# The seven-product second layer for two more token blocks of an attention and mixture-of-experts kernel

## The chip, the core and the metric

The kernel runs on one core of one Trainium2 chip. The metric is device time in microseconds for one execution, the median of several runs. Three runs of the kernel before took 1181.03, 1179.86 and 1181.36 us.

## What is computed

Linear attention (4 batches, 8 heads, 576 tokens, head size 64) gives 2304 tokens of width 512; a mixture of four experts and then an ELU network follow. Cut to what matters:

```python
kv = einsum("bhsd,bhse->bhde", softmax_k, v); x = einsum("bhsd,bhde->bhse", softmax_q, kv)   # -> (2304, 512)
for e in range(4):
    out += p[:, e:e+1] * (np.maximum(x @ w1[e], 0) @ w2[e])          # 512 -> 1024 -> 512
h = out @ w_in                                                        # float64 weights, 512 -> 2048
g = np.where(h > 0, h, np.exp(np.minimum(h, 0)) - 1.0)
return (g @ w_out).astype(np.float32)                                 # 2048 -> 512
```

## The kernel before, in words

**Number format.** Every matrix operand is split into a high part, rounded to the matmul format, and the rest (hi by a ScalarE Copy, lo by a subtraction on VectorE or GpSimd). One product of two split operands is three matmuls.

**Units, blocks, steps.** After the attention and the first expert, the work is ten units of 512 hidden columns, s = 0 to 9: 0 to 5 are the experts 1 to 3, 6 to 9 are the ELU network (`S_MOE` = 6; "sixth" in the change's name is this s = 6). Tokens are cut into three blocks b of 768. A step is (s, b), 30 in all. In step (s, b) TensorE runs the first layer of (s, b), 14 products named idx 0 to 13 (two halves `fp` of seven, a Strassen-like scheme of 7 products in place of 8), six matmuls each, and between them, at fixed places, the second layer of the step before.

**The second layer** has two forms. Units 0 to 4 and 7 to 9 (`SEVEN`) use seven products too. For units 7 to 9 this is `turned_product`: for each of the seven products in `TURNED`, 12 matmuls of 384 columns into a pair of PSUM banks, which VectorE then adds to the result (L1321). The transposed result lies in `accs`, in quarters (th, mh). Units 5 and 6 are plain. Unit 6 does eight `group`s (L1283 to L1286): 12 matmuls of 384 columns each, and one ScalarE Copy that writes the result's first value. The seven-product form needs sums of the four weight quarters (T1 to T4) and, of the hidden layer, the seven operands A11, A22, S1 to S4, A12 in place of eight plain parts; `fast(i)` says whether step i is of that form, and `elu` makes the operands with more VectorE sums and more conversions (`parts`, L1199 to L1201).

**PSUM.** Four banks A to D take the first layer's products. ScalarE copies out of them at idx 0 and 1 of each half (L1467, L1470), VectorE adds at idx 2 and 4 (L1474, L1485), then `elu` reads them. A product waits when its bank has not been read.

**The order.** All is written out by hand. Each step has 24 hooks; `hooks` says how many have run after which product. `at2(i, k, fn)` puts work on hook k of step i; a k of 24 or more reaches into the next steps. Engines run their own instructions in the order of the program, SP (and in places ScalarE) their DMAs, so that an instruction that waits holds those behind it.

**Other work on the hooks.** (a) `convert` turns a tile of the float64 weights `w_in`, `w_out` into float32 in the DRAM buffer `scratch`: load (L467, L469), five VectorE instructions (L487 to L506), one Exp, a store (L509); `CONV` lists the places of all 32. (b) `w_load`, `w1_steps`, `w2_step`, `w2_fast` load and split the weights of the next unit; the raw tiles are two slots of the pool `stg` (tag "r"), and split second-layer weights eight slots of `wp` (tag "w2"). (c) Between units 5 and 6 the expert result is turned: `turn_steps(b, c)` transposes two rows of 128 tokens (`turn`, L970), makes the operands T1 to T4, B11 to B22 and stores them to `xs[1]` (`emit`, L988 to L999), through staging places handed out in turn by `staged`; the next step's loads (`ring_load`, L719) read them in the second half of a step. One stream per (b, c), six items, one item after each product, at most two streams at once.

**What the change touches:** `TURNED`'s constants, `w2_parts`/`w2_sum` as called by `w2_fast`, `w2_step`, `CONV`, the loop that places `w_load`, `staged`, the places of `turn_steps`, `fast`, and `turned_product`.

Of the kernel before, what the change touches and what calls it, by code (L numbers as in the profile page):

```python
# [21 lines left out]
def tile_attention_moe_moe(  # L22
# [13 lines left out]
    nc = tc.nc  # L36
# [73 lines left out]
    )  # L110
    STARTS, ENDS = (0, 1, 5), (3, 4, 5, 6)
    GROUPS = tuple((th, m) for th in (1, 0) for m in range(4))
# [705 lines left out]
    def w2_sum(s, op):  # L818
# [4 lines left out]
        nc.vector.tensor_tensor(out=o, in0=x, in1=y, op=ALU.subtract)  # L823

    def w2_fast(i, s, d):

        for k, fn, op in (
            (8, w2_parts, "B11"), (16, w2_sum, "T1"), (17, w2_parts, "T1"), (18, w2_parts, "B22"), (19, w2_sum, "T3"),
            (20, w2_parts, "B21"), (22, w2_sum, "T2"), (24, w2_parts, "T2"), (30, w2_sum, "T4"), (31, w2_parts, "T3"),
            (35, w2_parts, "T4"),  # L830
        ) if s > S_MOE else (
            (8, w2_parts, "B11"), (13, w2_sum, "T1"), (17, w2_parts, "T1"), (18, w2_parts, "B22"), (19, w2_sum, "T3"),
            (21, w2_parts, "B21"), (22, w2_parts, "T3"), (24, w2_sum, "T2"), (26, w2_parts, "T2"), (27, w2_sum, "T4"),
            (30, w2_parts, "T4"),
        ):
            put = lambda k, fn: at2(i, k, fn) if k >= 0 else at(210 + k, fn)
            put(k - d, lambda fn=fn, op=op: fn(s, op))

    def w2_step(s, p):
        r = w2r.pop((s, p))  # L840
        for j in range(2):
            t = wp.tile([P, 2, DM], F32R, tag="w2", name="w2s")
            nc.scalar.activation(out=t[:, 0], in_=r[:, j], func=AF.Copy)
            nc.gpsimd.tensor_tensor(out=t[:, 1], in0=r[:, j], in1=t[:, 0].bitcast(F32), op=ALU.subtract)
            w2s[s, 2 * p + j] = t


# [4 lines left out]
    def at2(i, k, fn):  # L852
        timed2.setdefault(i * SH + int(k), []).append(fn)
# [16 lines left out]
    for n, fn in zip((190, 191, 192, 193, 194, 195, 197, 198, 200, 201), w1_steps(0, 0).values()):  # L870
# [11 lines left out]
        (later, SPELL * n + t, d, False)  # L882
        for n in range(S_FAST) for t, d in ((10, 2), (34, 1), (48, 1), (62, 1)) if (n, t) != (0, 10)
    ]
    CONV += [(later, end1 + t, 1, True) for t in (11, 22, 33)]
    end2 = NB * S_MOE * SH
    CONV += [(later, end2 + t, 1, True) for t in (42, 56)]
    assert len(CONV) == NCONV
# [4 lines left out]
    for i, (s, b) in enumerate(STEPS):  # L893
# [7 lines left out]
        if b == 0:  # L901

            a2, b2, c2, d2, a1, b1 = (2, 13, 25, 29, 34, 38)
            if s > 0 and (s <= S_FAST or SEVEN[s]):
# [4 lines left out]
                else:  # L909
                    at2(i, 14, lambda s=s: w2_step(s, 0))  # L910
                    at2(i, 19, lambda s=s: w2_step(s, 1))
                    a2, b2, c2, d2, a1, b1 = (23, 26, 30, 34, 38, 42)
            if s == S_MOE:
                a1, b1 = (42, 42)
            elif s > S_MOE:
                a1, b1 = (35, 40)
# [12 lines left out]

    stage, more_places = ["y", "qh", "ql", "extra", "ek"], []  # L930

    def staged():
# [9 lines left out]
        if now >= -SH and not more_places:  # L942
            y = gt.rearrange("p k n -> p (k n)").bitcast(F32R)
            more_places.extend(y[:, k * DM : (k + 1) * DM].rearrange("p (l n) -> p l n", l=2) for k in range(3))
            stage[:0] = more_places
        if now >= 0 and any(isinstance(t, str) for t in stage):
            stage[:] = two(stg, "r") + [t for t in stage if not isinstance(t, str)]
        if now >= 14 and len(stage) == 7:
            stage[:0] = two(stg, "r")
        t = stage.pop(0)  # L950
# [73 lines left out]
    for b in range(NB):  # L1024
        i = NB * (S_MOE - 1) + b + 1
        for c, n in enumerate((7, SH - 1, SH + 3)):
            f = turn_steps(b, c)
# [135 lines left out]
    def fast(i):  # L1163
        return 0 <= i < len(STEPS) and SEVEN[STEPS[i][0]]

# [129 lines left out]
    def turned_product(i, k):  # L1295
# [6 lines left out]
        op, wname, (th, mh) = TURNED[k]  # L1302
        t, y = w2g[s, wname], sums["XY"[(i + k) % 2]][:, :, :TB]
        last = i + 1 == len(STEPS)
        ym = [y[:, 0], (A, C)[k % 2]] if last else [y[:, 0], y[:, 1]]
        for m in range(2):
            n = 0
            for fp in range(2):
                gh, gl = parts_of(i, op, fp)
                w = t[:, :, fp, m * P : (m + 1) * P]  # L1310
                for l, r in ((w[:, 0], gh), (w[:, 1], gh), (w[:, 0], gl)):
# [7 lines left out]
        def add(ms, x):  # L1319
            a = acc_turned(b, th, mh)[:, ms]  # L1320
            nc.vector.tensor_tensor(out=a, in0=x, in1=a, op=ALU.add)  # L1321
            if s == STEPS[-1][0] and k in ENDS:
# [284 lines left out]
```

## Time and profile before

| | |
|---|---|
| median of 3 runs | 1181.03 us (1179.86 to 1181.36) |
| the profiled execution | 1180.01 us |
| its span, first to last instruction | 1178.2 us |
| TensorE clock granted | 1.00 throughout |
| instructions | 21091 |

In the profile PE is TensorE's matmuls, PEld its weight loads (one per matmul), DVE is VectorE, ACT ScalarE, POOL GpSimd, SP the queue that issues most DMAs. L1283 is line 1283 of the kernel before. A step begins with the first weight load of its idx 0; by that, the steps begin at 635.87 us (4,1), 725.09 (5,1), 827.32 (6,1), 859.66 (6,2), 890.86 (7,0), 951.49 (7,2) and 981.25 (8,0), and each ends where the next begins. A matmul's shown time overlaps the next one's, so TensorE's pace is read from the distance of the weight loads, not from the duration of one.

### The profile page before, as it was taken

The page shows a single profiled execution, that of the slowest core. Times are in us where ns is not written, and L with a number is a line of the kernel's source. Part 1 is how long each engine was busy: PE and PEld are TensorE (multiplying, and loading weights), DVE is VectorE, ACT ScalarE, POOL GpSimd, SP SyncE. Part 2 cuts the span into 40 slices and gives each one's busy share as a digit, 9 for nine tenths or more (in the row PEclk, how much of TensorE's full clock was granted, in tenths as well). Part 3 has the DMA queues.
Part 4 walks back from the last instruction along what each step waited for, and adds up shares of the span by engine and source line. Part 5 has one row for each costly group of instructions (what it writes and reads, how often), then busy time and mean ns, then how long its engine had stood idle before and what let it go on. Part 6 is the DMA issues. An engine that isn't in the chain of part 4 may idle for free.

```text
span 1178.2 us, 21091 instructions
## 1 busy us (share of the span) xinstructions
PE 1161.9 (99%) x7551; PEld 1113.6 (95%) x7551; DVE 883.9 (75%) x1533; ACT 656.1 (56%) x1410; POOL 604.1 (51%) x582
## 2 busy tenths in 40 slices
PE   8999999999999999999999999999999999999998
PEld 6889898889999999999999999998999999999998
DVE  7878887555787787787787786576566779879876
ACT  7554544236455455455455453356767766767763
POOL 6522543027468468468468463246534645645643
PEclk9999999999999999999999999999999999999999
DMA  9446666846767767767777658798985465565462
GB/s 270 144 144 191 192 211 222 287 166 224 259 233 251 259 233 251 258 233 250 253 239 251 241 208 311 259 340 279 335 320 188 181 230 198 196 229 198 176 242 108
DMA packets 150345, 272.76 MB, mean 231 GB/s; under 512 B 12640, under 2 KB 74848, under 8 KB 150240
## 3 DMA queue, kind: packets, MB, share of 16 engines
q1 hardware_dynamic: 148512, 268.26, 66.1%
q10 hardware_dynamic: 1728, 3.15, 0.8%
q8 instruction: 60, 0.98, 0.3%
q14 instruction: 45, 0.37, 0.1%
HBM read 225.22 MB, written 46.14 MB: 230 GB/s over the span
## 4 chain that ended last, share of the span: by engine, by line
PE 80%; DVE 5%; ACT 2%; issue 1%; POOL 1%; DMA 0%; DVEq 0%; POOLq 0%; ACTq 0%
PE o L1403 19%; PE m L1177 17%; PE h L1177 17%; PE o L1312 8%; PE h L1035 4%; PE o L1035 4%; PE o L1283 1%; PE o L1284 1%; PE o L1285 1%; PE o L1264 1%; PE o L1265 1%; PE o L1263 1%; DVE accs L1321 1%; PE o L970 1%; DVE w1s L777 1%
## 5 line engine op out<-in xcount | busy, mean ns | idle before, releaser
L1177 PE MATMUL m<-xh,w1s 128*128 128x384 f32 x840 | 245.9, 337 | 1.3 <-DVE h L1474 0.8
L1177 PE MATMUL h<-xh,w1s 128*128 128x384 f32 x840 | 244.8, 337 | 1.9 <-DVE half L1233 0.9
L1177 PEld LDWEIGHTS m<-xh,w1s 128*128 128x128 f32 x840 | 154.2, 188 | 6.1 <-DVE gt L1360 2.2
L1177 PEld LDWEIGHTS h<-xh,w1s 128*128 128x128 f32 x840 | 154.8, 188 | 5.1 <-DVE half L1233 1.5
L1177 PE MATMUL h<-xl,w1s 128*128 128x384 f32 x420 | 140.7, 335 | 0.0
L1177 PE MATMUL m<-xl,w1s 128*128 128x384 f32 x420 | 140.6, 335 | 0.0
L1035 PE MATMUL o<-w2t,hpa 128*128 128x512 f32 x432 | 117.1, 399 | 1.0 <-ACT hpa L1066 0.5
L1035 PE MATMUL h<-xh,w1t 128*128 128x256 f32 (+1 forms) x512 | 110.9, 295 | 0.0
L1403 PE MATMUL o<-w2g,xh 128*128 128x256 f32 x540 | 90.4, 282 | 0.0
L1035 PEld LDWEIGHTS o<-w2t,hpa 128*128 128x128 f32 x432 | 75.7, 189 | 14.8 <-DVE hpa L1067 1.9
L1035 PEld LDWEIGHTS h<-xh,w1t 128*128 128x128 f32 x512 | 85.0, 189 | 4.8
L1403 PE MATMUL o<-w2g,hpa 128*128 128x256 f32 x540 | 89.0, 282 | 0.0
L1403 PE MATMUL o<-w2g,xl 128*128 128x256 f32 x540 | 87.3, 282 | 0.0
L815 POOL TENSOR_TENSOR w2g<-r,w2g 128x512 fp32r<-128x512 f32 x56 | 74.8, 1344 | 24.2 <-ACT w2g L814 24.2
L1425 DVE SCALAR_TENSOR_TENSOR accs<-o,pn,accs 128x256 f32<-128x256 f32 x180 | 75.7, 475 | 14.7 <-PE o L1403 14.1
L1177 PEld LDWEIGHTS h<-xl,w1s 128*128 128x128 f32 x420 | 79.2, 189 | 0.3
L1177 PEld LDWEIGHTS m<-xl,w1s 128*128 128x128 f32 x420 | 78.9, 188 | 0.5
L1403 PEld LDWEIGHTS o<-w2g,xh 128*128 128x128 f32 x540 | 78.0, 190 | 0.1
L1035 PE MATMUL h<-xl,w1t 128*128 128x256 f32 (+1 forms) x256 | 77.0, 301 | 0.5 <-DVE xl L413 0.5
L1403 PEld LDWEIGHTS o<-w2g,hpa 128*128 128x128 f32 x540 | 76.1, 190 | 0.1
L1403 PEld LDWEIGHTS o<-w2g,xl 128*128 128x128 f32 x540 | 75.7, 190 | 0.1
L1201 POOL TENSOR_TENSOR hpa<-gt,hpa 128x384 fp32r<-128x384 f32 x28 | 28.5, 1020 | 75.3 <-ACT hpa L1199 75.3
(357 smaller groups left out, 2960.3 us busy)
## 6 DMA issues: line engine op xcount, KB each, us to landing
xh<-xs SPq DMA_DIRECT2D x210, 384.0 KB, 5.5
xl<-xs SPq DMA_DIRECT2D x210, 384.0 KB, 6.1
r<-in_w_dram SPq DMA_DIRECT2D x56, 256.0 KB, 4.8
xs<-xh SPq DMA_DIRECT2D x21, 384.0 KB, 4.6
xs<-xl SPq DMA_DIRECT2D x21, 384.0 KB, 4.4
xs<-stage SPq DMA_DIRECT2D x29, 256.0 KB, 5.1
r<-scratch SPq DMA_DIRECT2D x24, 256.0 KB, 4.2
xs<-gt SPq DMA_DIRECT2D x21, 256.0 KB, 4.5
```

What stands on the lines that cost most here:

```text
L777: eng.tensor_tensor(out=dst(k, 1), in0=src(k), in1=dst(k, 0).bitcast(F32), op=ALU.subtract)
L815: nc.gpsimd.tensor_tensor(out=t[:, 1], in0=src, in1=t[:, 0].bitcast(F32), op=ALU.subtract)
L970: nc.tensor.transpose(t[:, d * P : (d + 1) * P], a[:, d * P : (d + 1) * P], ident)
L1035: nc.tensor.matmul(out, lhsT, rhs, **kw)
L1177: nc.tensor.matmul(dst, t[:, wl, c + dl, :], x[xl_][:, dl, :], start=(n == 0 and p < 2), stop=(n == 5), skip_group_check=True,)
L1201: eng.tensor_tensor(out=gl, in0=g, in1=gh.bitcast(F32), op=ALU.subtract)
L1263: nc.tensor.matmul(o, gh, w[:, 0, :], start=(f == 0), stop=False)
L1264: nc.tensor.matmul(o, gh, w[:, 1, :], start=False, stop=False)
L1265: nc.tensor.matmul(o, gl, w[:, 0, :], start=False, stop=(f == FS - 1))
L1312: nc.tensor.matmul(ym[m], l, r, start=(n == 0 and k in STARTS), stop=(n == 5), skip_group_check=True)
L1403: nc.tensor.matmul(o, l, r, start=(first_write and m == 0 and c != 1), stop=(m == 5), skip_group_check=True)
L1425: nc.vector.scalar_tensor_tensor(out=a, in0=sums[x][:, c * HALF_M : (c + 1) * HALF_M], scalar=pr, in1=a, op0=ALU.mult, op1=ALU.add)
```

## The change

Steps (6,1) and (6,2) become `fast`: their second layers, issued in steps (6,2) and (7,0), are seven products in place of eight groups. Block 0 of unit 6 stays plain, and so does all of unit 5.

- Products that are the first to write a quarter of the result (`OPENS`: the first, second, third and seventh) are written by a ScalarE Copy when s is 6; the other three are added by VectorE as in units 7 to 9.
- B11, B21, B22 are taken from the plain split tiles of unit 6 (`w2_of`). For T1 to T4, `sums_of` subtracts the raw quarters on VectorE three and four hooks after `w2_step`, in the raw tile itself, and stores it to a DRAM buffer; in step (6,1) four loads (hooks 1, 3, 5, 7) bring the sums into "w2" slots, and `sum_parts` splits them ten hooks or more later.
- Unit 7's second-layer weights are split at other hooks, so that their slots are free by then.
- Two conversions leave unit 6 (hooks 42 and 56 from its start); units 3 and 4 get five in place of four.
- The loads of unit 6's first-layer weights are issued at hooks 41 and 54 of (5,0) on, in place of 38 and 42.
- Block 2's second turn starts at hook 17 of step (6,0) in place of 23; near the end of that step `staged` gives up the three places in `gt` one by one and, from hook 4 of (6,1), all but the four places in the raw slots.

```diff
-    STARTS, ENDS = (0, 1, 5), (3, 4, 5, 6)
+    STARTS, ENDS, OPENS = (0, 1, 5), (3, 4, 5, 6), (0, 1, 2, 6)
...
+    sums_dram = nc.dram_tensor("sums", (2, P, 2, DM), F32).ap()
+    SUM_HOME = {"T1": (0, 0), "T3": (0, 1), "T2": (1, 1), "T4": (1, 0)}
+
+    def sums_of(r, j, last):
+        b11, b12, b21, b22 = (r[:, a, c * HALF_M : (c + 1) * HALF_M] for a in range(2) for c in range(2))
+        for o, x, y in ((b22, b22, b11), (b21, b21, b22)) if last else ((b11, b12, b11), (b12, b12, b22)):
+            nc.vector.tensor_tensor(out=o, in0=x, in1=y, op=ALU.subtract)
+        if last:
+            nc.sync.dma_start(out=sums_dram[j], in_=r)
+
+    def sum_load(s, op):
+        a, c = SUM_HOME[op]
+        t = wp.tile([P, 2, 2, HALF_M], F32R, tag="w2", name="w2g")
+        src = sums_dram[:, :, a, c * HALF_M : (c + 1) * HALF_M].rearrange("j p n -> p j n")
+        nc.sync.dma_start(out=t[:, 1].bitcast(F32), in_=src)
+        w2g[s, op] = t
+
+    def sum_parts(s, op):
+        t = w2g[s, op]
+        nc.scalar.activation(out=t[:, 0], in_=t[:, 1].bitcast(F32), func=AF.Copy)
+        eng = nc.vector if op in ("T1", "T3") else nc.gpsimd
+        eng.tensor_tensor(out=t[:, 1], in0=t[:, 1].bitcast(F32), in1=t[:, 0].bitcast(F32), op=ALU.subtract)
+
+    def w2_of(s, op, fp, m):
+        ms = slice(m * P, (m + 1) * P)
+        if (s, op) in w2g:
+            return w2g[s, op][:, :, fp, ms]
+        a, c = int(op[1]) - 1, int(op[2]) - 1
+        return w2s[s, 2 * fp + a][:, :, c * HALF_M : (c + 1) * HALF_M][:, :, ms]
+
     def w2_fast(i, s, d):
         for k, fn, op in (
+            (8, w2_parts, "B11"), (16, w2_sum, "T1"), (21, w2_parts, "T1"), (22, w2_parts, "B22"), (23, w2_sum, "T3"),
+            (24, w2_sum, "T2"), (25, w2_parts, "T2"), (28, w2_parts, "B21"), (30, w2_sum, "T4"), (31, w2_parts, "T3"),
+            (35, w2_parts, "T4"),
+        ) if s == S_MOE + 1 else (
             (8, w2_parts, "B11"), (16, w2_sum, "T1"), (17, w2_parts, "T1"), (18, w2_parts, "B22"), (19, w2_sum, "T3"),
             (20, w2_parts, "B21"), (22, w2_sum, "T2"), (24, w2_parts, "T2"), (30, w2_sum, "T4"), (31, w2_parts, "T3"),
...
+        if s == S_MOE:
+            now = hook2_n[0] - NB * S_FAST * SH
+            for n in range(2):
+                at2(NB * S_FAST, now + 3 + n, lambda n=n: sums_of(r, p, n))
...
-        for n in range(S_FAST) for t, d in ((10, 2), (34, 1), (48, 1), (62, 1)) if (n, t) != (0, 10)
+        for n in range(S_FAST)
+        for t, d in (((10, 2), (34, 1), (48, 1), (62, 1)) if n < 3 else ((10, 2), (28, 1), (38, 1), (49, 1), (62, 1)))
+        if (n, t) != (0, 10)
     ]
     CONV += [(later, end1 + t, 1, True) for t in (11, 22, 33)]
-    end2 = NB * S_MOE * SH
-    CONV += [(later, end2 + t, 1, True) for t in (42, 56)]
...
-                    a2, b2, c2, d2, a1, b1 = (23, 26, 30, 34, 38, 42)
+                    a2, b2, c2, d2, a1, b1 = (23, 26, 30, 34, 41, 54)
             if s == S_MOE:
                 a1, b1 = (42, 42)
+                for hk, op in zip((1, 3, 5, 7), ("T1", "T2", "T3", "T4")):
+                    at2(i + 1, hk, lambda s=s, op=op: sum_load(s, op))
+                    at2(i + 1, 10 + 2 * hk, lambda s=s, op=op: sum_parts(s, op))
...
+        gone = more_places[: 1 if now < SH + 1 else 2 if now < SH + 4 else 3]
+        if now >= SH - 1:
+            stage[:] = [t for t in stage if not any(t is g for g in gone)]
+        if now >= SH + 4:
+            stage[:] = [t for t in stage if any(t is r for r in raw_places)]
...
-        for c, n in enumerate((7, SH - 1, SH + 3)):
+        for c, n in enumerate((7, SH - 1 if b < 2 else 17, SH + 3)):
...
     def fast(i):
-        return 0 <= i < len(STEPS) and SEVEN[STEPS[i][0]]
+        return 0 <= i < len(STEPS) and (SEVEN[STEPS[i][0]] or STEPS[i][0] == S_MOE and STEPS[i][1] > 0)
...
-        t, y = w2g[s, wname], sums["XY"[(i + k) % 2]][:, :, :TB]
+        y = sums["XY"[(i + k) % 2]][:, :, :TB]
...
-                w = t[:, :, fp, m * P : (m + 1) * P]
+                w = w2_of(s, wname, fp, m)
...
-            nc.vector.tensor_tensor(out=a, in0=x, in1=a, op=ALU.add)
+            if s == S_MOE and k in OPENS:
+                nc.scalar.activation(out=a, in_=x, func=AF.Copy)
+            else:
+                nc.vector.tensor_tensor(out=a, in0=x, in1=a, op=ALU.add)
```

## Rows read from the trace of the kernel before

**Rows 1.** The page, busy time, share of the span and count by engine.
```profile
PE 1161.9 (99%) x7551; PEld 1113.6 (95%) x7551; DVE 883.9 (75%) x1533; ACT 656.1 (56%) x1410; POOL 604.1 (51%) x582
```

**Rows 2.** Busy time by stretch, one line per step: (4,1), (5,1), (6,1), (6,2), (7,0), (7,2), (8,0).
```profile
core 0: us, PE busy (x) PEld busy (x) DVE busy (x) ACT busy (x) POOL busy (x), PEclk, DMA share, GB/s
635.87:665.50 29.63, 29.63 (x212) 29.63 (x211) 22.33 (x41) 15.57 (x33) 19.34 (x18) 1.00 0.70 248
725.09:758.53 33.44, 33.37 (x173) 29.93 (x173) 20.48 (x37) 12.64 (x26) 8.36 (x8) 1.00 0.76 265
827.32:859.66 32.34, 32.34 (x191) 32.00 (x189) 17.66 (x31) 23.93 (x55) 17.37 (x21) 1.00 1.01 344
859.66:890.86 31.20, 31.20 (x182) 31.20 (x181) 17.94 (x32) 21.83 (x50) 9.91 (x11) 1.00 0.85 311
890.86:922.06 31.20, 31.20 (x182) 31.20 (x181) 20.57 (x35) 23.81 (x56) 16.31 (x15) 1.00 0.59 209
951.49:981.25 29.76, 29.43 (x170) 29.11 (x170) 24.30 (x43) 20.15 (x46) 13.59 (x15) 1.00 0.62 229
981.25:1011.76 30.51, 29.67 (x170) 29.03 (x169) 28.95 (x47) 22.28 (x51) 17.87 (x17) 1.00 0.58 204
```

**Rows 3.** Timeline of PEld: start us, us; 24 loads from the first shown to the second.
```profile
859.66 0.19 PEld L1177 LDWEIGHTS m<-xh,w1s 128*128 128x128 f32 x1
...
863.82 0.19 PEld L1177 LDWEIGHTS m<-xh,w1s 128*128 128x128 f32 x1
```

**Rows 4.** Waits of PEld in (7,2), then in (8,0): us in total, times, longest.
```profile
PEld h L1177 <- DVE m L1474: 0.7, 1, 0.7
...
PEld h L1177 <- DVE half L1233: 0.8, 1, 0.8
PEld m L1177 <- DVE h L1474: 0.7, 1, 0.7
```

**Rows 5.** Timeline of DVE in (7,2) and (8,0); in brackets idle time before and its end.
```profile
964.02 0.95 DVE L1321 TENSOR_TENSOR accs<-o,accs 128x768 f32<-128x768 f32 x1
965.25 0.57 DVE L1227 SCALAR_TENSOR_TENSOR h<-h,half 128x384 f32<-128x384 f32 x1 [0.28 <-ACT extra L1217]
...
984.76 0.95 DVE L1321 TENSOR_TENSOR accs<-o,accs 128x768 f32<-128x768 f32 x1
...
987.50 1.12 DVE L783 TENSOR_TENSOR r<-r 128x256 f32<-128x256 f32 x1
...
989.69 0.55 DVE L1474 TENSOR_TENSOR h<-m,extra 128x384 f32<-128x384 f32 x1
```

**Rows 6.** Groups of instructions by form, whole span: busy us, mean ns, idle before.
```profile
L1201 POOL TENSOR_TENSOR hpa<-gt,hpa 128x384 fp32r<-128x384 f32 x28 | 28.5, 1020 | 75.3 <-ACT hpa L1199 75.3
...
L1411 ACT ACTIVATE m<-o 128x768 f32<-128x768 f32 x15 | 12.0, 803 | 6.8 <-PE o L1403 6.8
```

**Rows 7.** DMA issues of the whole span: KB each, median us from issue to landing.
```profile
xs<-stage SPq DMA_DIRECT2D x29, 256.0 KB, 5.1
```

**Rows 8.** Timeline of DVE in (6,1): a write into a staging place.
```profile
834.06 1.22 DVE L999 TENSOR_TENSOR stage<-accs,stage 128x512 fp32r<-128x512 f32 x1 [0.58 <-DMA xs<-stage]
```

**Rows 9.** Groups by form, whole span: the five VectorE instructions of a conversion.
```profile
L493 DVE TENSOR_SCALAR y<-x 128x512 int32<-128x512 int32 x19 | 20.5, 1077 | 0.0
L497 DVE SCALAR_TENSOR_TENSOR y<-x,y 128x512 f32<-128x512 uint32 x19 | 19.2, 1013 | 0.3
L506 DVE SCALAR_TENSOR_TENSOR y<-y,ce 128x512 f32<-128x512 f32 x19 | 16.7, 878 | 0.3
L487 DVE TENSOR_SCALAR ce<-x 128x512 uint16<-128x512 uint16 x19 | 14.4, 759 | 2.4 <-DMA x<-in_w_out_dram 2.3
L503 DVE SCALAR_TENSOR_TENSOR ce<-x,ce 128x512 uint16<-128x512 uint16 x19 | 12.9, 680 | 0.0
```

**Rows 10.** Line L782 (a subtraction of 128x256): ns min/median/max, first and last start.
```profile
L782 DVE TENSOR_TENSOR r<-r x18: 415/776/1399, 242.8 to 1076.3; 128x256 f32<-128x256 f32 x18
```

**Rows 11.** Landing of the DMAs of the DRAM buffer `scratch`, all of them.
```profile
DMA to landing us min/median/max: 2.1/4.9/8.5
```

More of the change, by code (lines that the diff above doesn't have):

```diff
@@ L927, in tile_attention_moe_moe @@
                 at2(i, 13 + n, fn)
-    stage, more_places = ["y", "qh", "ql", "extra", "ek"], []
+    stage, more_places, raw_places = ["y", "qh", "ql", "extra", "ek"], [], []
     def staged():
@@ L945, in staged @@
             stage[:0] = more_places
[L946 to L949, printed above, removed]
+        if now >= 0 and not raw_places:
+            raw_places.extend(two(stg, "r"))
+            stage[:] = raw_places + [t for t in stage if not isinstance(t, str)]
+        if now >= 14 and len(raw_places) == 2:
+            raw_places.extend(two(stg, "r"))
+            stage[:0] = raw_places[2:]
+        gone = more_places[: 1 if now < SH + 1 else 2 if now < SH + 4 else 3]
[3 more added lines that the diff above has]
+            stage[:] = [t for t in stage if any(t is r for r in raw_places)]
         t = stage.pop(0)
```

## The prediction

> **What bounds the kernel now.** The page comes first: TensorE's matmuls cover 99% of the span [rows 1], the other engines at most 75%. Matmul times overlap, so the second view is the table by stretch, one line per step, with the weight loads (PEld) beside them [rows 2]. In steps (6,2) and (7,0) the loads fill all 31.20 us: TensorE takes its next instruction without a pause. In (7,2) and (8,0), which have a seven-product layer on both sides, the steps last 29.76 and 30.51 us. Third, the pace: between two weight loads that are 24 loads apart lie 863.82 - 859.66 = 4.16 us [rows 3], so one 128x384 matmul costs 0.1733 us; 180 of them are 31.20 us, which is just step (6,2). Fourth, where the seven-product steps lose time: 168 matmuls would be 29.12 us, so (7,2) loses 0.64 and (8,0) 1.39 us. The waits of the weight loads name one stop of 0.7 us in (7,2) and two of 0.8 and 0.7 us in (8,0), each on a VectorE instruction that empties a PSUM bank [rows 4]. So the path is TensorE's queue everywhere, and VectorE's order is what interrupts it.
>
> **What leaves TensorE.** A plain second layer is 8 groups of 12 matmuls, 96; seven products of 12 are 84. Two blocks: 24 matmuls fewer of 384 columns, at 0.1733 us -4.16 us. It comes off steps (6,2) and (7,0), where the second layers of blocks 1 and 2 are issued. Both are full of weight loads today, so nothing else holds these 4.16 us; what follows is what other engines give back.
>
> **Step (6,2).** It gets the form of (7,2): seven products of the block before beside its own seven-product first layer. The stop in (7,2) comes out of a VectorE queue that was idle at 965.25 us for 0.28 us [rows 5] and from there works without a break up to the late L1474 behind which TensorE waits. The additions of the first three products lie before that idle moment, the last of them at 964.02 us; the new Copy for first writes takes them off VectorE, but the idle moment already separates them from the stop. I take +0.65; ends 0 (no stop, as in today's (6,2)) and 1.4 (as in (8,0)).
>
> **Step (7,0).** It gets the form of (8,0), with one difference: the four products that open a quarter go through ScalarE (Copy of 128x768, nearest row 0.80 us [rows 6]) instead of VectorE (0.95 us, the addition at 964.02 [rows 5]). In (8,0) VectorE works without a break from the addition at 984.76 to the L1474 at 989.69 that came 0.7 us late [rows 5]. That addition belongs to the seventh product of the block before, one of the four: without its 0.95 us the first stop is gone, and with the next two gone also (2.8 us in all) the second of 0.8 us. VectorE loses 3.8 of 28.95 us, ScalarE gains 3.2 on 22.28 of 30.51 us and stays under 26. I take +0.3, nearer to the free end, because both stops stand behind work that leaves; ends 0 and 1.39.
>
> **Step (6,1).** Its PE work stays: 96 group matmuls, 84 of the first layer, the turning of one row pair. Its own first layer becomes seven-product: four sums per half on VectorE, and three more conversions per half on ScalarE and GpSimd (1.02 us each there [rows 6]), part of them in the next step. The conversion of a 64-bit tile that lay here leaves (4.4 us, below). (7,0) of today has this mix, groups beside a seven-product first layer: VectorE is busy 20.57 us, GpSimd 16.31, and nothing is lost at 31.20 us [rows 2]. So load does not decide. New is that the last turn has four staging places where it had nine: seven stagings follow one another, and the place is rewritten two products and one group later, 24 matmuls or 4.16 us, while a store lands in 5.1 us [rows 7]. VectorE then waits about 1 us in its queue; behind it stand the sums of the A21 quarter, for which TensorE's second half waits. In the trace such a wait is seen once, 0.58 us [rows 8], and costs no stop. Against it, the second-last turn is now done before this step. I take +0.3; ends -0.3 (the small stop there is now goes) and +2.
>
> **Conversions.** Two of the 64-bit to 32-bit conversions move from unit 6 to units 3 and 4. One is five VectorE instructions, 0.76 + 1.08 + 1.01 + 0.68 + 0.88 = 4.41 us [rows 9]. In units 3 and 4 the middle step then holds two: (4,1) has 22.33 us of VectorE in 29.63 [rows 2], so 26.7, 90%; that is under (8,0)'s 95%, which loses 1.39, and over (7,2)'s 82%. Their loads stand in SP's queue: the third's load is issued one hook before the second's last read of the same buffer, so SP stands still for that read, about a hook; the ring loads behind it begin only with the step's second half, so nothing waits. The store of a result lands about 4 to 5 us after its issue and the buffer is rewritten two products and a fill later, so VectorE may wait some tenths. I take +0.2 for both units; ends 0 and 2 x 1.39 = 2.8.
>
> **Sums and their traffic.** Eight subtractions of 128x256 in (5,1): 0.415 to 1.40 us each [rows 10], 3.3 to 11.2 us in a step where VectorE is idle 13 us of 33.44 [rows 2]: 0. They wait for GpSimd's four subtractions of the raw weights; GpSimd is busy 8.36 us there. Two stores and four loads of 256 to 512 KB on SP replace two loads and two stores of conversions: 0. The two weight loads of layer one are on ScalarE's queue; the first now also waits for the store of the sums issued seven hooks before it (a hook is a 24th of a step, 1.4 us), 9.8 us, longer than a landing of 4.9 us, 8.5 at most [rows 11]: 0, upper end 0.7 (one stop, as in [rows 4]), since ScalarE's evacuations stand behind it. The other one moves 12 hooks later, still 13 hooks ahead of its reader. The four new conversions of the sums (ScalarE, then VectorE or GpSimd) lie in (6,1), ten hooks behind their loads: 0. Unit 7's conversions move one to eight hooks back, each still ahead of its product; the T2 subtraction then follows the B22 conversion it must wait for by two hooks, and VectorE may wait there; its next deadline is three products away: 0, upper end again one stop, 0.7.
>
> **Sum.** -4.16 + 0.65 + 0.3 + 0.3 + 0.2 = -2.71 us, 0.23%. The profiled execution took 1180.01 us (1178.2 of span and 1.8 around it) and would take 1177.3; the runs shown have their median at 1181.03, 1.0 above it, and lie within 1.5 us. I give the forecast for the median: 1178.3. About 0.2%, 2.4 us, is what a measurement of this kernel can tell from no change, so the forecast lies just beyond it.
>
> **The rivals.**
> All covered (0.20): the stops of (6,2) and (6,1) do not come. For it: (4,1) runs full with VectorE at 75% [rows 2], and (7,2)'s 24.30 us less three additions would be 74%. Against it: the stop of (7,2) lies behind the idle moment. Then -4.16, 1176.9.
>
> VectorE stays the brake in (7,0) (0.20): GpSimd's conversions lengthen VectorE's reads. In (8,0) the L783 at 987.50 took 1.12 us, and L782, of the same shape, takes between 0.415 and 1.40 [rows 5, 10]. If freed time is eaten this way, (7,0) loses 1.39 instead of 0.3, and -1.6 remains: 1179.4. Against it: the removed additions stand in the queue before the stops. The Trainium skill (SBUF — State Buffer, section "Who interferes with whom") has a VectorE instruction with two SBUF inputs shut out while GpSimd reads SBUF, for the whole of that instruction; the spread of L782 agrees with it, and by that rule every GpSimd conversion this change adds would count against it.
>
> The moved conversions stall units 3 and 4 (0.12): at 90% VectorE both steps lose what (8,0) loses, 2.8 instead of 0.2: 1180.9, no change. Against it: in (4,1) the queue has 7.3 us of idle time today [rows 2].
>
> Staging makes it slower (0.08): in (6,1) two rewrites wait for a landing. If a store takes 7.4 us or more, each wait is 3.3 us or more, and two of them in a chain outweigh the 4.16 and 2.4 more; at the longest landing on SP's queue that I found, 8.5 us [rows 11], it is 2 x 4.3 = 8.7 us and 1186.7 us. At the decisive point: about 1183.4. For it: DMA is fully busy there (share 1.01 [rows 2]). Against it: the median of 5.1 us, and the 1 to 2 us by which the bank evacuations may be late.
>
> **The numbers.** The forecast's own case has 0.40. Its spread (0.7 us with the measurement's) puts a quarter of it on the near side of 0.2%. Faster by over 0.2%: 0.30 + 0.20 + some of the VectorE case, 0.55; within 0.2%: 0.37; slower: 0.08. The range of 8 in 10 leaves out the slow tail and the best corner (all covered and the small stops gone too): 1176.4 to 1180.9.
>
> **What would show it.** Right: L1312's weight loads rise by 168 and the groups' fall by 192; (6,2) near 29.8 and (7,0) near 29.4 us; (6,1) within half a us of 32.3; (3,1) and (4,1) still 29.6 to 29.8; a wait of VectorE's L999 on the DMA xs<-stage of about 1 us in (6,1). Wrong: (7,0) above 30.2 with waits on L1474 or L1233; (4,1) above 30; weight loads stopped in the second half of (6,1) or, if the last store is late, at the third product of (6,2); an idle ScalarE in front of the weight load at the end of (5,1).

## The result, and the profile after

The changed kernel is slower: 1195.31 us median (1191.73 to 1197.62) against 1181.03 (1179.86 to 1181.63), ratio 1.0116 with a 95% interval of 1.0094 to 1.0137. The forecast was 1178.3, its range ended at 1180.9, and the longest price among its rivals was 1186.7: none of them holds the result. The profiled execution took 1197.62 us, the longest of the five, with a span of 1195.8, 17.6 us more than the span before; so the steps below hold some 3 us more than lies between the medians.

The page's busy line, which answers to [rows 1]:

```profile
PE 1167.1 (98%) x7527; PEld 1114.7 (93%) x7527; DVE 907.5 (76%) x1569; ACT 662.2 (55%) x1418; POOL 616.5 (52%) x592
```

The 24 matmuls are gone (7551 before, 7527 now), but their busy time rose by 5 us and the share fell. So matmuls stopped, and some ran longer. Next the busy time by stretch, one line per step: two steps of the kernel before that have no row above, (3,2) and (4,2):

```profile
576.01:605.75 29.74, 29.74 (x211) 29.66 (x211) 24.54 (x41) 15.23 (x32) 14.55 (x15) 1.00 0.72 244
665.50:695.13 29.63, 29.63 (x211) 29.63 (x211) 24.53 (x41) 15.11 (x32) 14.82 (x15) 1.00 0.69 244
```

and the changed kernel's steps (3,2), (4,2), (6,1), (6,2) and (7,0); the last three answer to [rows 2]. Columns as there: length, then busy time of PE, PEld, DVE, ACT, POOL, the granted clock, the DMA share, GB/s.

```profile
577.29:613.80 36.51, 32.67 (x211) 32.31 (x211) 24.41 (x44) 15.74 (x33) 14.68 (x15) 0.91 0.65 231
673.83:707.60 33.77, 31.40 (x211) 31.08 (x211) 24.37 (x44) 15.63 (x33) 15.23 (x15) 0.95 0.68 246
839.83:878.90 39.07, 34.60 (x190) 33.52 (x190) 20.98 (x35) 25.91 (x59) 20.81 (x24) 0.96 0.87 288
878.90:909.16 30.26, 29.70 (x170) 29.06 (x170) 21.66 (x40) 23.41 (x53) 15.61 (x16) 1.00 0.80 293
909.16:939.07 29.91, 29.40 (x170) 29.08 (x169) 26.03 (x44) 23.98 (x53) 15.36 (x15) 1.00 0.57 202
```

Three steps hold the loss: (3,2) +6.77, (4,2) +4.14, (6,1) +6.73 us, 17.6 in all. (6,2) and (7,0) do give time back, 0.94 + 1.29 = 2.23 us; the remaining 2.2 us are tenths in other steps and around them ((9,2) +0.44, (3,1) and (4,1) +0.3 each). Of the five, it is in these three that the granted clock is under 1.

What stopped (3,2) stands in VectorE's timeline, and its consequence in that of the weight loads (start, us, instruction; in brackets the idle time before and what ended it):

```profile
583.26 0.43 DVE L487 TENSOR_SCALAR ce<-x 128x512 uint16<-128x512 uint16 x1 [2.87 <-DMA x<-in_w_in_dram]
587.86 0.81 DVE L493 TENSOR_SCALAR y<-x 128x512 int32<-128x512 int32 x1 [4.17 <-DMA scratch<-y]
588.71 0.69 DVE L497 SCALAR_TENSOR_TENSOR y<-x,y 128x512 f32<-128x512 uint32 x1
589.32 0.56 DVE L1525 TENSOR_TENSOR h<-m,extra 128x384 f32<-128x384 f32 x1
```
```profile
589.93 0.28 PEld L1225 LDWEIGHTS m<-xh,w1s 128*128 128x128 f32 x1 [4.16 <-DVE h L1525]
590.09 0.33 PEld L1225 LDWEIGHTS m<-xl,w1s 128*128 128x128 f32 x1
...
597.04 0.19 PEld L1225 LDWEIGHTS m<-xl,w1s 128*128 128x128 f32 x1
```

The moved conversion waits twice in VectorE's queue: 2.87 us for its own load, then 4.17 us until the result of the conversion before it has left `y`. The evacuation at L1525 (L1474 before) stands behind it, and TensorE waits 4.16 us for that. Afterwards loads come every 0.33 us, and again every 0.18 us from about 596 us. The table by stretch names the reason (the clock is the third column from the end):

```profile
585.00:590.00 5.00, 1.16 (x8) 0.84 (x6) 2.11 (x4) 2.18 (x4) 0.99 (x1) 0.93 0.07 27
590.00:595.00 5.00, 5.00 (x21) 5.00 (x21) 2.28 (x4) 1.39 (x3) 0.00 (x0) 0.50 0.69 209
595.00:600.00 5.00, 5.00 (x34) 5.00 (x34) 3.91 (x7) 2.14 (x6) 1.54 (x2) 0.88 0.26 106
```

After this stop TensorE runs at 0.50, the lower of its two levels (1.2 instead of 2.4 GHz), for 6.8 us. About half of that is lost on top of the stop: TensorE's busy time in the step is 32.67 us, where it was 29.74 for the same 211 matmuls. (4,2) repeats it with 1.87 and 4.10 us of VectorE's waits, a stop of 2.69 us and 3.4 us at the half clock.

Why so long? The landing times of the transfers issued from 574 to 579.5 us (KB each, median us from issue to landing):

```profile
xh<-xs SPq DMA_DIRECT2D x2, 384.0 KB, 9.1
xl<-xs SPq DMA_DIRECT2D x2, 384.0 KB, 9.3
x<-in_w_in_dram SPq DMA_DIRECT2D x1, 512.0 KB, 8.7
scratch<-y SPq DMA_DIRECT2D x1, 256.0 KB, 9.1
```

The conversion's load and the store of the result before it stand among and behind the ring's loads on SyncE, the DMA engines are full (405 GB/s in this stretch), and everything takes some 9 us to land. The change itself crowds the queue: SyncE stood still for 10.6 us ahead of the load at 561.97 us, until VectorE's L503 had read `x` for the conversion before (SyncE's timeline, two issues that follow each other):

```profile
551.07 0.32 SPq L509 DMA_DIRECT2D scratch<-y  x1
561.97 0.33 SPq L469 DMA_DIRECT2D x<-in_w_out_dram  x1
```

Fourteen ring loads, which the kernel before issues from 552.74 to 574.28 us, therefore all lie between 565.21 and 577.73 us. How much of the 9.1 us this makes was not tested. The Trainium skill (SBUF — State Buffer, section "The DMA setup-cost knee") fits a transfer as about 2 us plus its bytes at 436 GB/s, an estimate of 2.6 us for 256 KB. The trace agrees for a store that the kernel before issued at 583.64 us, when the DMA engines were nearly idle (share 0.07): 2.4 us. It doesn't agree for the store here, which stands behind a full queue: 9.1 us.

In (6,1) TensorE stops twice. The first stop, 3.15 us, is behind ScalarE, which waits for GpSimd; the second, 1.93 us, is behind VectorE, which twice waits for a staging place's store to land. ScalarE, the weight loads at the first stop, then VectorE:

```profile
846.46 0.63 ACT L1036 ACTIVATE stage<-accs 128x512 fp32r<-128x512 f32 x1 [3.54 <-POOL accs L1053]
847.00 0.47 ACT L1521 ACTIVATE h<-m 128x384 f32<-128x384 f32 x1
```
```profile
847.52 0.19 PEld L1225 LDWEIGHTS m<-xh,w1s 128*128 128x128 f32 x1 [3.15 <-ACT h L1521]
```
```profile
854.00 0.69 DVE L1047 TENSOR_TENSOR stage<-accs,stage 128x512 fp32r<-128x512 f32 x1 [4.55 <-DMA xs<-stage]
...
860.69 1.45 DVE L1047 TENSOR_TENSOR stage<-accs,stage 128x512 fp32r<-128x512 f32 x1 [2.36 <-DMA xs<-stage]
```

After the first of VectorE's two waits the engine is idle again, 0.85 us ahead of 855.53, so it is the second that stands right ahead of the late sums. The bank copy L1521 (L1470 before) stands behind a staging copy L1036 (L988), whose source GpSimd's subtractions L1053 (L1005) are still writing. It is the turn that the change moved from hook 23 to hook 17. The half clock follows the first stop too (3.4 us).

In (7,0) only one of (8,0)'s two stops [rows 4] is there, 0.83 us behind L1525. VectorE's timeline just ahead of it, with two rows of the same work behind GpSimd's last conversion (which ends at 917.5 us):

```profile
914.29 1.19 DVE L782 TENSOR_TENSOR r<-r 128x256 f32<-128x256 f32 x1
915.51 1.12 DVE L783 TENSOR_TENSOR r<-r 128x256 f32<-128x256 f32 x1
916.56 1.23 DVE L777 TENSOR_TENSOR w1s<-r,w1s 128x256 fp32r<-128x256 f32 x1
917.71 0.55 DVE L1525 TENSOR_TENSOR h<-m,extra 128x384 f32<-128x384 f32 x1
918.18 0.41 DVE L788 TENSOR_TENSOR r<-r 128x256 f32<-128x256 f32 x1
918.62 0.42 DVE L789 TENSOR_TENSOR r<-r 128x256 f32<-128x256 f32 x1
```

Subtractions of the same 128x256 take 1.1 to 1.2 us while GpSimd converts and 0.4 after it: by these rows part of the freed VectorE time was eaten so, which no run tested.

### The profile page after: what moved, and what is told of

Read it like the earlier page. It is cut to its first block, busy times and chain, and to the rows that moved or that the text cites. A ratio compares the mean times of both kernels' runs of the same rounds, so it can differ in the third digit from the quotient of the medians.

```text
span 1195.8 us, 21148 instructions
## 1 busy us (share of the span) xinstructions
PE 1167.1 (98%) x7527; PEld 1114.7 (93%) x7527; DVE 907.5 (76%) x1569; ACT 662.2 (55%) x1418; POOL 616.5 (52%) x592
## 3 DMA queue, kind: packets, MB, share of 16 engines
q10 hardware_dynamic: 1728, 3.15, 0.7%
## 4 chain that ended last, share of the span: by engine, by line
PE 65%; DVE 10%; DMA 5%; ACT 4%; POOL 3%; issue 2%; SPq 0%; DVEq 0%; POOLq 0%; ACTq 0%
PE o L1454 15%; PE m L1225 13%; PE h L1225 13%; PE o L1360 9%; PE h L1083 4%; PE o L1083 4%; DMA xl<-xs 2%; DMA scratch<-y 1%; PE o L1312 1%; PE o L1313 1%; PE o L1311 1%; DMA xs<-stage 1%; POOL w2g L815 1%; DVE accs L1372 1%; DVE w1s L777 1%
```

## The experiments

Each kernel was timed beside the kernel before on the same chip (its medians 1180.89 to 1181.09). Step lengths and stretches at the half clock are of the profiled execution, in us:

| kernel | median | ratio, 95% | (3,2) | (4,2) | (6,1) | (6,2) | (7,0) | half clock in these steps |
|---|---|---|---|---|---|---|---|---|
| before | 1181.03 | | 29.74 | 29.63 | 32.34 | 31.20 | 31.20 | none |
| changed | 1195.31 | 1.0116 [1.0094, 1.0137] | 36.51 | 33.77 | 39.07 | 30.26 | 29.91 | 6.8, 3.4, 3.4 |
| 1 conversions alone | 1189.29 | 1.0068 [1.0045, 1.0092] | 33.65 | 33.97 | 32.31 | 31.20 | 31.20 | 3.4, 3.4 |
| 2 result place apart | 1186.59 | 1.0048 [1.0033, 1.0063] | 29.89 | 29.89 | 39.66 | 30.27 | 29.83 | 3.4 |
| 3 turn alone | 1185.40 | 1.0042 [1.0027, 1.0058] | 29.63 | 29.63 | 37.41 | 31.20 | 31.20 | 3.4 |
| 4 turn at hook 14 | 1193.64 | 1.0112 [1.0089, 1.0134] | 34.87 | 35.98 | 39.11 | 30.27 | 29.80 | 3.4, 6.8, 3.4 |
| 5 nine places | 1183.98 | 1.0024 [1.0014, 1.0033] | 29.87 | 29.87 | 36.40 | 30.24 | 29.91 | 3.4 |
| 6 late turn, four places | 1187.57 | 1.0057 [1.0037, 1.0077] | 29.87 | 29.86 | 39.90 | 30.27 | 29.81 | 6.8 |
| 7 sums on GpSimd | 1184.10 | 1.0029 [1.0018, 1.0040] | 29.87 | 29.87 | 36.52 | 29.75 | 29.81 | 3.4 |
| 8 wider conversions | 1187.95 | 1.0060 [1.0045, 1.0075] | 31.07 | 31.04 | 35.47 | 30.39 | 29.79 | none |
| 9 late loads | 1183.99 | 1.0026 [1.0014, 1.0037] | 29.87 | 29.87 | 33.56 | 31.94 | 29.91 | none |
| 10 late loads, sums on GpSimd | 1182.39 | 1.0013 [1.0004, 1.0022] | 29.89 | 29.87 | 33.29 | 32.41 | 29.93 | none |
| 11 later divisions | 1183.27 | 1.0017 [1.0008, 1.0026] | 29.87 | 29.87 | 33.93 | 31.49 | 29.91 | none |
| 12 loads on ScalarE's queue | 1184.98 | 1.0031 [1.0021, 1.0041] | 29.86 | 29.89 | 36.41 | 30.27 | 29.91 | 3.4 |

**1. The conversions alone.** The kernel before, with only the list of conversions changed:

```diff
-        for n in range(S_FAST) for t, d in ((10, 2), (34, 1), (48, 1), (62, 1)) if (n, t) != (0, 10)
+        for n in range(S_FAST)
+        for t, d in (((10, 2), (34, 1), (48, 1), (62, 1)) if n < 3 else ((10, 2), (28, 1), (38, 1), (49, 1), (62, 1)))
+        if (n, t) != (0, 10)
...
-    CONV += [(later, end2 + t, 1, True) for t in (42, 56)]
```

> The kernel before, with only the conversions moved from unit 6 to units 3 and 4. Theory C (two DMA waits in VectorE's queue, for the load of the third conversion's input and for the store of the second one's result, each behind the ring loads): steps (3,2) and (4,2) last 36.5 and 33.8 us as in the changed kernel, about +10.9 us, 1192 us. Rival R (the moved conversions harm only because other parts of the change load the queues as well): both steps at 29.6 to 30.0 us and 1181 to 1182 us.

VectorE waited for `y` twice, and both stops and half-clock stretches came, of 2.64 and 2.76 us. The waits in (3,2) to (4,2), total, times and longest:

```profile
DVE y L493 <- DMA scratch<-y: 8.6, 2, 4.4
PEld m L1177 <- DVE h L1474: 5.4, 2, 2.8
DVE ce L487 <- DMA x<-in_w_in_dram: 1.7, 1, 1.7
DVE ce L487 <- DMA x<-in_w_out_dram: 1.6, 1, 1.6
```

So this part alone costs about 8 us, less than the 11 expected, since (3,2) took 33.65 us and not 36.5. The runs of this kernel lie 9 us apart, and the longer ones had the lower granted clock (1183.91 us at 1.000, 1192.78 at 0.994); what makes them differ was not tested.

**2. A place of its own for one result.** The changed kernel; the conversion at hook 49 of units 3 and 4, which lies in (3,2) and (4,2), writes to another place than the one at hook 38 ahead of it, so that it needn't wait for that store:

```diff
-        for n, fn in zip(..., convert(s, aside)):
+        for n, fn in zip(..., convert(s, aside, t % SPELL == 49)):
...
+            elif apart:
+                t["y"] = extra[:, TB : TB + DM]
```

> The changed kernel; the third of the close conversions writes its result into another place, so that it need not wait for the second one's store. Theory C: VectorE's wait of 4.2 and 4.1 us on that store is gone, the wait of 1.9 to 2.9 us on the load stays and is covered; (3,2) and (4,2) fall to about 30 us, the clock stays at 1.00 there, about -10.5 us against the changed kernel: 1185. Rival V (VectorE's amount of work in units 3 and 4 is what costs): unchanged, 1195.

Both steps fell to 29.89 us at full clock. All that is left of the conversion's waits there is its load:

```profile
DVE ce L489 <- DMA x<-in_w_in_dram: 1.4, 1, 1.4
...
DVE ce L489 <- DMA x<-in_w_out_dram: 0.4, 1, 0.4
```

The work on VectorE is the same as in the changed kernel, and the store at 576.75 us still landed only after 8.5 us. So the wait for the store did it, not the load of VectorE at 24 to 25 of 30 us.

**3. The early turn alone.** The kernel before, with the second turn of block 2 at hook 17:

```diff
-        for c, n in enumerate((7, SH - 1, SH + 3)):
+        for c, n in enumerate((7, SH - 1 if b < 2 else 17, SH + 3)):
```

> The kernel before, with only block 2's second turn started at hook 17 in place of 23. Theory P (the earlier turn puts ScalarE's wait for GpSimd's subtractions right ahead of the copy that frees the bank at idx 1 of (6,1), a stop of 3.15 us and a slower clock after it): (6,1) near 36.5 us, 1185 us. Rival S (the four staging places make all of (6,1)'s loss): (6,1) at 32.3 us or below, 1181 us.

The same stop of 3.15 us came, with the half clock behind it. The waits in (6,1) and the stretch after the stop:

```profile
PEld m L1177 <- ACT h L1470: 3.1, 1, 3.1
...
ACT stage L988 <- POOL accs L1005: 5.3, 2, 3.5
```
```profile
836.00:839.40 3.40, 3.40 (x16) 3.29 (x15) 0.57 (x1) 1.67 (x3) 0.54 (x1) 0.50 0.99 319
```

The early turn costs 5 us of (6,1) by itself, 4.3 between the medians: the stop and half of 3.4 us.

**4. The turn three hooks earlier still.** The changed kernel with hook 14 in place of 17.

> The changed kernel with block 2's second turn one product earlier (hook 14 for 17). Theory P: the wait for GpSimd falls to the last product of (6,0), where no bank copy stands behind it; the stop at idx 1 of (6,1) and its slower clock go, (6,1) falls from 39.1 to about 34.5 us, 1190.8 us. Rival S: (6,1) stays at 38 to 39 us, 1195 us.

A miss: the stop behind ScalarE went, but (6,1) stayed at 39.1 us, as rival S had it. There are two other stops. One of 2.62 us is new, behind VectorE's sums, whose queue waited 2.1 us for a staging place. The one of 2.85 us, where the changed kernel has 1.93, is behind sums that waited 4.0 us for GpSimd's part of a staging. So the turn was one brake, and staging is the next that these rows name.

**5. The turn back, and nine places.** Kernel 2 with the turn at hook 23 again and a written list for the places: three in `gt`, four in the turning pool, two in `ek`, ordered so that those that are needed for the next layer's parts are used first.

```diff
-        stage[:] = [t for t in stage if any(t is r for r in raw_places)]
...
+        planned.extend([g[0], g[1], r[0], r[1], k[0], k[1], g[2], r[2], r[3], r[0], r[1], k[0], r[2], r[3]])
+        stage[:] = planned
```

> The kernel of the result-place run (third close conversion writes apart), with block 2's second turn back at hook 23 and nine staging places for the last two turns, handed out in a written order (three in gt before its first use, two in ek of which one is free again for the sum S4, four raw). Theory P (the early turn and the four places make (6,1)'s loss, through ScalarE's wait for GpSimd and VectorE's wait for a landing): (6,1) 32.3 to 33 us, 1179 to 1180 us. Rival Q (the four loads of the sums, 1 MB more in a step whose DMA is full, make every landing late): (6,1) above 34.5 us, 1182 us or more.

Q's forecast came: (6,1) 36.40 us, 1183.98 in all, and one stop of 2.8 us. Against kernel 2 the step still fell by 3.3 us, so the turn and the places had their part. VectorE, ScalarE and GpSimd all waited for landings there:

```profile
DVE stage L1050 <- DMA xs<-stage: 3.0, 2, 2.3
PEld h L1228 <- DVE half L1284: 2.8, 1, 2.8
...
ACT stage L1039 <- DMA xs<-stage: 2.3, 1, 2.3
...
POOL stage L1041 <- DMA xs<-stage: 2.0, 1, 2.0
```

**6. The turn back, with the four places of the change.** Kernel 2 with the turn at hook 23.

> The kernel of the result-place run with only the second turn back at hook 23, the staging rule as in the change (four places from hook 4 of (6,1) on). Theory P: the stop behind ScalarE's wait at idx 1 goes, but two turns share four places, and VectorE's waits for landings grow: (6,1) 38 to 41 us, 1186 to 1188 us. Rival S' (the early turn alone is to blame): (6,1) about 34.5 us, 1182 us.

One stop of 5.53 us behind the sums (two runs): with four places the late turn is no better than the early one (39.90 us against kernel 2's 39.66), which fits the miss of kernel 4. Kernel 3 shows that the early turn also costs 5 us with the places of the kernel before. So (6,1) seems to need both cures, though the early turn with nine places was not run in the changed kernel.

**7. All formed sums divided on GpSimd.** Kernel 5 with `eng = nc.gpsimd` for all four divisions.

> The run with more places, and T1 and T3 split on GpSimd as T2 and T4 are. If VectorE's wait of 1.7 us for ScalarE ahead of T3's subtraction is what makes its last sums late at the start of (6,2): the stop of 0.55 us there goes, about 0.5 us less than the run with more places. If not: the same time.

The stop of 0.55 us in (6,2) went (30.24 to 29.75), and the whole is the same as kernel 5's within its interval.

**8. Conversions further apart.** Kernel 5 with one result place again, and (10, 28, 42, 56, 70) as the hooks in units 3 and 4.

> The run with more places, but all conversions of units 3 and 4 write one place again and begin at hooks 10, 28, 42, 56 and 70, 14 apart. Theory C (it is the distance between a store and the next rewrite, and between a load and its use, against landings of up to 9 us): no wait of VectorE over 1 us on these DMAs, (3,2) and (4,2) within 30.2 us, the same time as the run with more places within 1 us. Rival V (five conversions in a unit are too much work for VectorE): 3 us or more above it.

A miss: by the time, 4.0 us above kernel 5, it is rival V's forecast that came. VectorE waits for no DMA in these steps any more, and the clock holds, but (3,2), (4,0), (4,2) and (5,0) are each 1.2 to 1.4 us longer than in the kernel before: conversions now lie where VectorE has no idle time, and its queue reaches an evacuation late:

```profile
596.62 1.24 DVE L784 TENSOR_TENSOR r<-r 128x256 f32<-128x256 f32 x1
597.89 1.12 DVE L785 TENSOR_TENSOR r<-r 128x256 f32<-128x256 f32 x1
598.93 0.68 DVE L505 SCALAR_TENSOR_TENSOR ce<-x,ce 128x512 uint16<-128x512 uint16 x1
599.64 0.69 DVE L508 SCALAR_TENSOR_TENSOR y<-y,ce 128x512 f32<-128x512 f32 x1
...
601.76 0.56 DVE L1528 TENSOR_TENSOR m<-h,extra 128x384 f32<-128x384 f32 x1
```

TensorE stopped 1.12 us behind that L1528. The amount of work alone is not it: kernel 5 has the same five conversions at other hooks, and its (3,2) and (4,2) take 29.87 us. Where they find VectorE without idle time they cost 1.2 to 1.4 us per step, near the 1.39 of the prediction; with the wait for a store they cost 3.9 to 6.8.

**9 and 10. The sums' loads later.** Kernels 5 and 7; the loads lie at hooks 12 to 18 instead of 1 to 7:

```diff
-                for hk, op in zip((1, 3, 5, 7), ("T1", "T2", "T3", "T4")):
+                for hk, kp, op in zip((12, 14, 16, 18), (18, 21, 24, 30), ("T1", "T2", "T3", "T4")):
                     at2(i + 1, hk, lambda s=s, op=op: sum_load(s, op))
-                    at2(i + 1, 10 + 2 * hk, lambda s=s, op=op: sum_parts(s, op))
+                    at2(i + 1, kp, lambda s=s, op=op: sum_parts(s, op))
```

> Kernel: the one with the separate result place, the turn back at hook 23 and the nine written staging places (1183.98 us, step (6,1) 36.40), with the four loads of the formed sums at hooks 12, 14, 16 and 18 of step (6,1) instead of 1, 3, 5 and 7, and their divisions at 18, 21, 24 and 30 instead of 12, 16, 20 and 24. In that kernel the stretch 830 to 850 us moved 348 GB/s with the queue's packets filling all 16 engines, 1 MB of it the sums' loads; VectorE, ScalarE and GpSimd each waited 2.0 to 2.3 us there for a staging place's store to land (843 to 846 us), then came the stop of 2.82 us and the half clock of 3.4 us. Theory Q (the loads' traffic and their places in SyncE's queue delay the stores): the waits on staging places fall under 1 us, the stop goes, the clock holds, (6,1) 32.3 to 33.2, whole kernel 1179.7 to 1181.0. Rival P' (it is the count of places and the order of the list; the loads only lie beside it): the waits stay near 2 us, the stop stays over 2 us with the half clock behind it, (6,1) 36 to 37, 1183.5 to 1185. Rival L (the late loads are themselves late): a stop at the start of (6,2) before the product with T1 or T2, (6,2) over 31.5.

> Kernel: as the one before (late loads), and all four formed sums divided on GpSimd. Theory Q and the division's measured 0.5 us in (6,2): (6,1) 32.3 to 33.2 and (6,2) 29.6 to 29.9, whole kernel 1179.2 to 1180.6. Rival P': (6,1) 36 to 37, 1183.5 to 1185. Rival L: GpSimd's division of T1 (1.6 us or more, behind its second-layer parts) comes late for the product at the start of (6,2), (6,2) over 30.5.

In both the waits for staging places fell to 0.8 us or less, the half clock went, and (6,1) came to 33.56 and 33.29 us, just above Q's range: the 1 MB of the sums had delayed the stores, as Q said. In 9, from 830 to 880 us:

```profile
ACT stage L1039 <- DMA xs<-stage: 0.8, 1, 0.8
```

But the whole kernel gained only in 10 (1.7 us against kernel 7, with intervals that just overlap), since (6,2) gave much of it back: 31.94 and 32.41. L is there as well, and Q's forecast of the total failed in both. In 10 ScalarE's copy waits for a load, and TensorE for ScalarE (waits from 830 to 880 us):

```profile
ACT w2g L846 <- DMA w2g<-sums: 2.8, 2, 2.0
...
PEld m L1228 <- ACT h L1524: 1.4, 1, 1.4
```

**11. The divisions later too.** Kernel 10 with (18, 24, 30, 36).

> Kernel: as e10 (nine staging places, loads of the sums at hooks 12, 14, 16 and 18, all four divided on GpSimd), with the divisions at 18, 24, 30 and 36 instead of 18, 21, 24 and 30. In e10 ScalarE waited 0.76 and 2.04 us for two of the loads to land (862.9 and 867.7 us, issued 855.8 and 858.2 us), and step (6,2) took 32.41 us with stops of 1.38 and 1.61 us. Theory L (the division's copy stands on ScalarE ahead of the second layer's steps and waits for a load still in the queue): ScalarE's waits for the sums fall under 0.3 us, the stop of 1.38 us goes, (6,2) 30.0 to 31.0, whole kernel 1180.3 to 1181.8. Rival T (the stops in (6,2) come from how the engines' work falls together, not from the loads): (6,2) stays over 31.8, 1182 to 1183.5.

Half of L: ScalarE waits for no load and the stop of 1.4 us went, but (6,2) is 31.49, between the two forecasts, and the total of 1183.27 is T's. A stop of 1.63 us behind VectorE stayed, as T said, and one of 0.72 us behind a ring load came. Kernels 10 and 11 do not differ by more than their intervals.

**12. The same loads on another queue.** Kernel 5, with `nc.scalar.dma_start` for the sums' loads.

> Kernel: as e5 (nine places, sums loaded at hooks 1, 3, 5 and 7 and divided at 12, 16, 20 and 24 on VectorE and GpSimd), but the four loads are issued on ScalarE's DMA queue instead of SyncE's. It parts theory Q in two. Q1, the traffic: the 16 DMA engines are full in that stretch (348 GB/s), so 1 MB more delays the stores whichever queue it is issued on: the waits for staging places stay near 2 us, the stop of 2.8 us and the half clock stay, (6,1) 35.5 to 37, whole kernel 1183.2 to 1185. Q2, the place in SyncE's queue: the loads wait their turn beside the stores and the stores land sooner; the waits fall under 1 us and (6,1) is 32.3 to 34, whole kernel 1179.8 to 1181.8. Either way ScalarE may lose some tenths of a us to issuing four transfers.

The stop (2.94 us), the half clock and (6,1) (36.41) are those of kernel 5. The waits moved: those for staging places fell to 1 us, which Q1 had not foretold, but the store out of `gt` landed late instead, and the four loads landed no sooner than on SyncE (6.5 us against 6.2). From 834 to 878 us the waits, and from 830 to 850 us the queues (packets, MB, share of 16 engines):

```profile
DVE gt L1279 <- DMA xs<-gt: 2.6, 1, 2.6
```
```profile
q1 hardware_dynamic: 6928, 5.81, 86.5%
q10 hardware_dynamic: 1088, 1.05, 15.1%
```

In kernel 5 the one queue had 102.8% there. So, by the time of the step, it is the traffic (Q1), not the order in one queue. The Trainium skill says as much (DMA: Bandwidth & Descriptors, section "Issuing engines are not separate DMA queues"): queues of different engines run on the same 16 DMA engines. The trace agrees: the two shares add up to 101.6%.

No version beat the kernel before; kernel 10 comes nearest, 1.5 us above it. It has the same 24 matmuls fewer; (7,0) keeps its gain, -1.27, and what keeps the kernel above is (6,1) +0.95, (6,2) +1.21 and tenths elsewhere. Not tried: the early turn with nine places, and the sums' loads split between both times.

## Why the prediction was wrong

- **What leaves TensorE (-4.16).** Right in kind: 24 matmuls fewer, and (6,2) and (7,0) show it.
- **(6,2) (+0.65) and (7,0) (+0.3).** Mis-sized. 168 matmuls are 29.12 us, so they lost 1.14 and 0.79 us. (6,2) has the foretold stop of 0.65 us and one of 0.55 that was not foretold, behind the sums' division on VectorE; kernel 7 took that away. (7,0) keeps one of two stops; ahead of it VectorE's subtractions stretch beside GpSimd, but that they are the cause is argued from the rows. The rival of VectorE as the brake named this mechanism; (7,0) lost 0.79 of its 1.39 us.
- **Conversions (+0.2, end 2.8): the step that failed most, +10.9 us.** The step priced VectorE's load by its share (90%) and took it as the risk. The failing sentences are "SP stands still for that read, about a hook; the ring loads behind it begin only with the step's second half, so nothing waits" and "the store of a result lands about 4 to 5 us after its issue ..., so VectorE may wait some tenths". SyncE stood still for 10.6 us, the ring's loads then filled the queue ahead of the next conversion, and load and store land in 8.7 and 9.1 us. The longest landing of [rows 11], 8.5 us, stood in the prediction, but was used for staging and not here. The rival of the moved conversions had the right units with the wrong step and the wrong cause: it priced the middle steps, where the work falls, but (3,1) and (4,1) lost 0.3 us each and the loss came one step later; and kernel 2 keeps the VectorE work and loses 0.15 and 0.26 us in (3,2) and (4,2).
- **(6,1) (+0.3, ends -0.3 and +2): +6.7 us.** The move of the second-last turn was taken as a relief ("against it, the second-last turn is now done before this step"). Kernel 3 shows it alone to cost 5 us, through a wait of ScalarE for GpSimd that the step never walked through: the bank copy behind a staging copy. The staging waits, foretold as about 1 us, were 4.55 and 2.36. The staging rival had that mechanism and priced it at up to 8.7 us; it got 0.08. Its two prices start from different sums: 1186.7 holds the forecast's other terms, 1183.4 only the -4.16, and with the other terms a landing of 7.4 us gives about 1184.5.
- **Sums and their traffic (0).** Failed: "two stores and four loads ... replace two loads and two stores of conversions: 0" compares bytes over the unit. The loads fall into the stretch where the DMA engines are full [rows 2], and kernels 5 and 9, and 7 and 10, put their price at 2.8 and 3.2 us of (6,1).
- **Left out altogether: the granted clock.** The sum let a stop cost its own length. With each of the three long stops the clock went to the lower level, 13.6 us in all, worth about 7 of the 17.6 us of the profiled execution: TensorE's busy time in the three steps rose by 2.9, 1.8 and 2.3 us. That (6,1) would be as much shorter without it is not shown (see the last section).

Of the 14.3 us between the medians, kernel 2 takes back 8.7 (conversions), kernel 5 another 2.6 (in (6,1)) and kernel 10 another 1.6 ((6,1) -3.1, (6,2) +2.2 by the profiles, the rest within the spread of the runs). The remaining 1.5 us hold the stops of (6,2). Why (9,2) is about 0.45 us longer in most of the kernels with the new products was not tested.

## What to carry over

Price a moved step by the DMAs that it waits for, at the landing time of the stretch that it moves into and not by the median of the span, and ask which store must land before its buffer is written again. Where the DMA share is already 1, added bytes are not free on any queue. A stop of TensorE that the lower clock follows can cost half of that stretch on top, so a wait of 3 us may cost 5, as in kernel 3; kernel 5's runs show that not all of it need come back where the clock holds.

## What the runs showed of the hardware

The clock fell with short stops, but not with each. TensorE had been busy up to the stop every time. The changed kernel and the twelve others show 21 stops over 1.5 us between 270 and 1120 us. Eleven came with 0.50 for 3.4 us (ten of 2.64 to 3.15 us and one of 3.77), three with 6.8 us (3.81, 4.16 and 5.53 us); the fall came between 1.7 us ahead of the stop's end and 1.3 us behind it. Three of like length came with none: 3.15 us in kernel 2, 2.62 in kernel 4 and 2.78 in kernel 8; and so did the four of 1.61 to 1.93 us. So the same stop of 3.15 us in (6,1) cost the lower clock in the changed kernel and in kernel 3, and not in kernel 2; there the second stop of the step was longer, 2.77 us against 1.93, the lower clock came with that one, and the step took no less (39.66 against 39.07 us). Kernel 5 fits that: its two runs at a granted clock of 1.000 took 1183.22 and 1184.21 us, one below and one above its median of 1183.98. In most of the new kernels there is also one stretch of 3.4 us in the first 35 us of the span; it lies ahead of everything that the change touches.

How late a store of 256 KB lands goes here with what is queued ahead of it. Within the same 20 us of unit 3 the kernel before has two: one issued at 570.20 us among the ring's loads lands in 7.0 us, one at 583.64 us, with the DMA engines nearly idle, in 2.4. In the changed kernel the store at 578.76 us, behind the last of the ring's loads, lands in 9.1 us.
